# Deep cross network on one core: where the bias vectors are loaded and summed, and the first and third input transposes in column tiles

## The chip, the cores and the metric

One core of a Trainium2 chip runs the whole kernel. The metric is the device time of one execution in microseconds (us). The time given for a kernel is the median of its runs; the profile comes from one of those runs.

## The reference

```python
    B, F, D, L = 4096, 26, 16, 6
    Din = min(F * D, 1024)
...
        "x0": _w((lambda *s: _rng.normal(s) * 0.05)(B, Din)),
        "ws": _w((lambda *s: _rng.normal(s) * 0.05)(L, Din, Din)),
        "bs": _w((lambda *s: _rng.normal(s) * 0.05)(L, Din)),
...
def reference(x0, ws, bs):
    x = x0
    for l in range(ws.shape[0]):
        x = x0 * (x @ ws[l] + bs[l]) + x
    return x
```

So `x0` has 4096 rows of 416 features, and six layers each take a 416 x 416 product, add a bias, multiply by `x0` and add the layer's input. All tensors are bf16.

## The kernel before, in words

The 4096 rows are worked through in four stages of 1024 rows (`NS`), each in two halves of 512 (`H`), and for each stage in six layers (`L`). The work is kept transposed: features on partitions, rows along the free dimension. The 416 features are three full chunks of 128 (`NC`) and a tail of 32 (`DR`), whose rows lie four groups deep on the partitions. In PSUM the products of all layers so far add up, so a layer's result is `x0` times (the sum in the bank plus the sum of the biases up to that layer). These sums of the biases, for every layer at once, are what `cb_sb` holds.

Every engine has its own order of work, written out by hand, and the engines meet at semaphores. The order at the start of the program, around the change:

- TensorE runs 40 warm-up matmuls on a constant (L130), in groups of four 128x32 column tiles. Then `bias_sums` (L295 to L303) waits for the load of the biases and multiplies `bsa_sb` (a row of ones and six rows of biases) by the triangular `u_sb`: 16 small matmuls into bank 1. Then `fill(1)` adds four more warm-up matmuls. The loop at L308 transposes the first two pairs of 128-row blocks of x, three chunks each, in the order `IN_ORDER`: 12 full 128x128 transposes (L312) into bf16 views of PSUM banks (`psT`).
- In the first layer of the first stage (`n == 0`, L355 to L367) the matmuls run chunk by chunk, `k` outside and `m` inside. `before_a` waits until the transposed inputs have been copied to SBUF. At `k == 0, m == 1` TensorE waits until `cb_sb` has been copied out of bank 1. At `k == 2, m == 1` it transposes the tail features (`tail_inputs`) and the third pair of blocks (`third_input`), both as ordinary matmuls by the identity in column tiles, with float32 results. The matmuls at L265 are all those that go through the helper `tile_mm`.
- Then come the row matmuls of the tail (L393 and L409), for which TensorE waits on the copies of the third input (`s_inD`, `s_inA`), on the copied tail (`s_te`) and on the small weights `wt_sb` and `wc_sb`.
- VectorE first clears `wc_sb` and writes the ones of `bsa_sb` (L141, L142), then copies the bias sums to `cb_sb` (L506), the first inputs' chunks 0 and 2 (L512), and chunks 0 and 2 of the third input (L517).
- ScalarE (ACT) copies chunk 1 of each (L561, L578) and the tail inputs (L576).
- Loads: SP's queue issues the biases (L134), the first and the third pair of x blocks (L135, L136), later a DMA transpose of the fourth pair (L158) and the weights. ACT's queue issues the second pair of x blocks (L137), the first layer's weights (L138), the tail features of the fourth pair (L139) and two pieces of `wt_sb`. GpSimd's queue (POOL) builds the identity and `u_sb` (L211, L215) and then issues two pieces of `wt_sb` (L125) and four of `wc_sb` (L206).

Semaphores that the steps below name: `s_bs` (biases landed), `s_zero` (VectorE's memsets), `s_set` (identity and `u_sb`), `s_xin` (x blocks landed), `s_inT` (a chunk transposed), `s_inD` and `s_inA` (a chunk copied by VectorE or ACT), `s_cbp` and `s_cb` (bias sums made and copied).

Of the kernel before, what the change touches and what calls it, by code (L numbers as in the profile page):

```python
# [8 lines left out]
ACTF = mybir.ActivationFunctionType  # L9


def bass_standalone__dcn_v2_cross__recsys_kernel(
# [8 lines left out]
    NC = 3  # L21
# [11 lines left out]
    with ExitStack() as es:  # L33
# [20 lines left out]
        o_sb = sb("o_sb", [128, NJ, D])  # L54
        ident = sb("ident", [128, 128])
        ones_sb = sb("ones_sb", [128, 256])
        bsa_sb = sb("bsa_sb", [L + 1, D])
        u_sb = sb("u_sb", [L + 1, L])
        cb_sb = sb("cb_sb", [128, NC + 1, L], FP32)
        cq_sb = sb("cq_sb", [128, NC + 2], FP32)  # L60
        ps = es.enter_context(nc.psum_tensor("ps", [128, 8, 512], FP32))
# [34 lines left out]


        IN_BANKS = ((3, 4, 6), (0, 5, 7))
        IN_ORDER = ((1, 0), (1, 1), (1, 2), (0, 0), (0, 1), (0, 2))
        THIRD = (3, 6, 7)  # L100

        NAT_BANKS = (0, 1, 2, 6, 7, 4, 3, 5)
# [23 lines left out]
                wt_sb[lane(g), a:b, 0:n1 - n0], ws[a:b, DF:D, n0:n1].rearrange("l p n -> p l n")  # L126
            ).then_inc(done, 16)

        for q in range(4 * 10):
            nc.tensor.matmul(  # L130
                ps[lane(q % 4), 7, 0:256], lhsT=CONST[:, 0:32], rhs=CONST, start=True, stop=True,
                skip_group_check=True, tile_position=(0, 32 * (q % 4)),
            )
        nc.sync.dma_start(bsa_sb[1:L + 1, :], bs[:, :]).then_inc(s_bs, 16)  # L134
        nc.sync.dma_start(xin_sb[:, 0:2, :], x0_w[:, 0, :, :]).then_inc(s_xin[0], 16)  # L135
        nc.sync.dma_start(xin_sb[:, 4:6, :], x0_w[:, 2, :, :]).then_inc(s_xin[2], 16)  # L136
        nc.scalar.dma_start(xin_sb[:, 2:4, :], x0_w[:, 1, :, :]).then_inc(s_xin[1], 16)  # L137
        nc.scalar.dma_start(w_sb[:, 0, :, :], wmain(0)).then_inc(s_w[0], 16)  # L138
        nc.scalar.dma_start(xtl_sb[:, :, :], x0_v[:, 6:JS, DF:D]).then_inc(s_xtl0, 16)  # L139
        nc.gpsimd.memset(ones_sb[:, :], 1.0).then_inc(s_ones, 1)  # L140
        nc.vector.memset(wc_sb[:, :, :], 0.0).then_inc(s_zero, 1)  # L141
        nc.vector.memset(bsa_sb[0:1, :], 1.0).then_inc(s_zero, 1)  # L142

        es2 = ExitStack()
# [57 lines left out]
        @block.gpsimd  # L202
        def _(pool):
            def load_wc(i, g):
                a, b = ((0, 1), (1, L))[i]
                pool.dma_start(  # L206
                    wc_sb[lane(g), a:b, 32 * g:32 * g + 32], ws[a:b, DF:D, DF:D].rearrange("l p n -> p l n")
                ).then_inc(s_wc[i], 16)

            pool.wait_ge(s_ones, 1)  # L210
            pool.affine_select(  # L211
                out=ident[:, :], in_=ones_sb[:, 0:128], pattern=[[-1, 128]],
                compare_op=ALU.is_equal, fill=0.0, base=0, channel_multiplier=1,
            ).then_inc(s_set, 1)
            pool.affine_select(  # L215
                out=u_sb[:, :], in_=ones_sb[0:L + 1, 0:L], pattern=[[1, L]],
                compare_op=ALU.is_ge, fill=0.0, base=1, channel_multiplier=-1,
            ).then_inc(s_set, 1)
            for g in (0, 2):
                load_wt(pool, g, 0, 1, s_wtp)  # L220
            pool.wait_ge(s_zero, 1)
            for i in range(2):
                for g in (1, 3):
                    load_wc(i, g)

            for s in range(NS):
                pool.wait_ge(s_te, s + 1)
                for l in range(L):
                    n = s * L + l + 1
                    if n == NL:  # L230
                        break
                    if n == 1:
                        pool.tensor_scalar(
                            out=cq_sb[:, 0:NC + 1], in0=cb_sb[:, :, L - 1], scalar1=-1.0, scalar2=None, op0=ALU.add
                        ).then_inc(s_cq, 1)
                        pool.wait_ge(s_cq, 1)
                        pool.tensor_tensor(
                            out=cq_sb[:, NC + 1:NC + 2], in0=cq_sb[:, NC:NC + 1], in1=cb_sb[:, NC, L - 2:L - 1], op=ALU.subtract
                        ).then_inc(s_cq, 1)
                    pool.wait_ge(s_ta, n)  # L240
                    dst = xot_sb[:, s, :] if l == L - 1 else xt_sb[:, (l + 1) % 2, 0:G]
                    pool.tensor_tensor(  # L242
                        out=dst, in0=t32_sb[:, n % 2, :], in1=x0t_sb[:, s, 0:G], op=ALU.mult
                    ).then_inc(s_xt, 1)
                    if n == NL - 1:
                        pool.tensor_scalar(
                            out=xot_sb[:, s, :], in0=t32_sb[:, n % 2, :], scalar1=cq_sb[:, NC + 1:NC + 2], scalar2=None, op0=ALU.add
                        ).then_inc(s_qt, 1)
                    if l == 2 and s > 0:
                        pool.wait_ge(s_ot, 16 * s)  # L250
                        pool.tensor_copy(
                            out=o_sb[:, (s - 1) * JS:s * JS, DF:D].rearrange("p (g r) f -> p r g f", r=2),
                            in_=ot_sb[:, s - 1, :, :].rearrange("p r (g f) -> p r g f", f=DR),
                        ).then_inc(s_otc, 1)
            pool.wait_ge(s_x0n, 16)
            for i, t in enumerate(POOL_TILES):
                pool.wait_ge(s_oA, i + 1)
                pool.tensor_tensor(
                    out=o_sb[:, j0 + t, :], in0=a32_sb[:, i, :], in1=x0n_sb[:, t, :], op=ALU.mult
                ).then_inc(s_oP, 1)  # L260

        @block.tensor
        def _(pe):
# [3 lines left out]
                    skip_group_check=True, tile_position=(0, 32 * q),  # L267
                )

            def fill(n):  # L270
                for i in range(n):
                    for q in range(4):
                        tile_mm(ps[lane(q), 7, 0:256], CONST[:, 0:32], CONST, q, True)

            def tail_inputs():
                for r in range(2):
# [7 lines left out]
            def third_input():  # L284
                pe.wait_ge(s_inD, 4)
                for c in range(NC):
                    for j in range(2):
                        for q in range(4):
                            f0 = c * 128 + 32 * q
                            ins = tile_mm(  # L290
                                ps[lane(q), THIRD[c], j * 128:j * 128 + 128], xin_sb[:, 4 + j, f0:f0 + 32], ident[:, :], q, True
                            )
                    ins.then_inc(s_inT, 1)

            def bias_sums():  # L295
                pe.wait_ge(s_bs, 16)
                pe.wait_ge(s_zero, 2)
                pe.wait_ge(s_set, 2)
                for c in range(NC + 1):
                    for q in range(4):  # L300
                        f0 = c * 128 + 32 * q if c < NC else DF
                        ins = tile_mm(ps[lane(q), 1, c * 8:c * 8 + L], bsa_sb[:, f0:f0 + 32], u_sb[:, :], q, True)
                ins.then_inc(s_cbp, 1)  # L303

            bias_sums()
            fill(1)
            pe.wait_ge(s_set, 1)
            for i, (h, c) in enumerate(IN_ORDER):  # L308
                if c == 0:
                    pe.wait_ge(s_xin[h], 16)  # L310
                for j in range(2 * h, 2 * h + 2):
                    ins = pe.transpose(  # L312
                        out=psT[:, IN_BANKS[h][c], (j % 2) * 128:(j % 2 + 1) * 128],
                        in_=xin_sb[:, j, c * 128:(c + 1) * 128], identity=ident[:, :],
                    )
                ins.then_inc(s_inT, 1)

            for s in range(NS):
                for l in range(L):
# [26 lines left out]

                    def before_a(k):
                        if n == 0:
                            pe.wait_ge((s_inD, s_inA, s_inD)[k], (3, 2, 4)[k])
                        else:  # L350
                            pe.wait_ge(s_xa, NC * (n - 1) + k + 1)
                            if l == 0 and k == 0:
# [2 lines left out]
                    if n == 0:  # L355
                        pe.wait_ge(s_w[0], 16)
                        for k in range(NC):
                            before_a(k)
                            for m in range(NC):
                                if k == 0 and m == 1:  # L360
                                    pe.wait_ge(s_cb, 1)
                                if k == 2 and m == 1:
                                    pe.wait_ge(s_xin[2], 16)
                                    pe.wait_ge(s_xtl0, 16)
                                    tail_inputs()
# [136 lines left out]

        @block.vector
        def _(dve):
            dve.wait_ge(s_cbp, 1)
            dve.tensor_copy(  # L506
                out=cb_sb[:, :, :], in_=ps[:, 1, 0:8 * (NC + 1)].rearrange("p (c e) -> p c e", e=8)[:, :, 0:L],
            ).then_inc(s_cb, 1)
            for i, (h, c) in enumerate(IN_ORDER):
                if c != 1:  # L510
                    dve.wait_ge(s_inT, i + 1)
                    dve.tensor_copy(  # L512
                        out=x0T_sb[:, c, h * 256:(h + 1) * 256], in_=psT[:, IN_BANKS[h][c], 0:256]
                    ).then_inc(s_inD, 1)
            for c in (0, 2):
                dve.wait_ge(s_inT, 2 * NC + c + 1)
                dve.tensor_copy(out=x0T_sb[:, c, 512:768], in_=ps[:, THIRD[c], 0:G]).then_inc(s_inD, 1)  # L517
            dve.wait_ge(s_cb, 1)
            for s in range(NS):
                for l in range(L):  # L520
# [35 lines left out]
        def _(act):  # L556
# [18 lines left out]
            act.wait_ge(s_tp, 1)  # L575
            act.activation(out=x0t_sb[:, 0, :], in_=ps[:, 5, :], func=ACTF.Copy).then_inc(s_te, 1)  # L576
            act.wait_ge(s_inT, 2 * NC + 2)
            act.activation(out=x0T_sb[:, 1, 512:768], in_=ps[:, THIRD[1], 0:G], func=ACTF.Copy).then_inc(s_inA, 1)  # L578
            act.wait_ge(s_cb, 1)
            for s in range(NS):  # L580
                for l in range(L):
# [77 lines left out]
```

## Time and profile before

| What | Value |
|---|---|
| Median of 8 runs | 128.27 us (127.9 to 129.09) |
| The profiled execution's own time | 129.09 us |
| Its span, first to last instruction | 127.8 us |
| PE busy | 124.3 us (97%) |
| VectorE (DVE) busy | 99.9 us (78%) |
| ScalarE (ACT) busy | 67.6 us (53%) |
| GpSimd (POOL) busy | 24.1 us (19%) |
| Warm-up matmuls, L130, 40 of them | 0.83 to 3.16 us |
| First 12 transposes, L312 | start 3.63 us, 1.46 us long |
| First layer's first matmuls, L265 | start 5.13 us |
| First row matmul, L393 | start 8.81 us |

The span counts from the first to the last instruction of the execution; what is left to its own time lies around it. PE is TensorE's matmuls, PEld its weight loads, which overlap them; a matmul's duration includes its way through the array, so several lie on top of each other. A group's line gives the line of the kernel, the engine, the operation, output and inputs with shapes, how often, and the busy time; a square bracket gives the idle time of the engine ahead of it and what ended it. The shape 128*32 is a matmul on a column tile of 32 columns, and four such tiles run side by side.

### The profile page before, as it was taken

To read this page: it belongs to the slowest core of one execution; us is meant where nothing else is said; L and a number is where in the kernel's file an instruction comes from. 1 tells how busy PE (TensorE), PEld (TensorE's weight loads), DVE (VectorE), ACT (ScalarE), POOL (GpSimd) and SP (SyncE) were. 2 spreads that over 40 slices of the span, in tenths; PEclk is the share of its full clock that TensorE was granted. 3 is DMA by queue.
4 is the path that set the end of the run, shared out by engine and by line. 5 is a ranking of instruction groups with operands and counts; after the bars stand their busy time and mean duration, and the time that the engine had idled before them with its cause. 6 is when DMAs were issued, how large, how long until landed. Compare 5 with 4: busy or idle time off the path is not lost.

```text
span 127.8 us, 5323 instructions
## 1 busy us (share of the span) xinstructions
PE 124.3 (97%) x2410; PEld 62.8 (49%) x2410; DVE 99.9 (78%) x154; ACT 67.6 (53%) x146; POOL 24.1 (19%) x44
## 2 busy tenths in 40 slices
PE   7999999999999999999999999999999999999991
PEld 5655445445445445445445454444444454454660
DVE  2329779789788798797797797797797797797973
ACT  0625555575744564575753573575762564566830
POOL 7512012022022023022022022121020120220441
DMA  3950799900009969450005889960006910430006
GB/s 110 269 133 5 161 241 241 152 5 0 5 3 48 213 100 232 116 204 5 0 5 111 155 115 233 313 215 0 5 0 47 206 24 0 155 117 5 0 25 246
DMA packets 31889, 13.49 MB, mean 106 GB/s; under 512 B 24950, under 2 KB 31868, under 8 KB 31868
## 3 DMA queue, kind: packets, MB, share of 16 engines
q1 hardware_dynamic: 30476, 12.12, 44.8%
q10 hardware_dynamic: 1200, 0.99, 2.4%
q8 instruction: 19, 0.31, 1.0%
q0 software_dynamic: 192, 0.06, 0.3%
q14 instruction: 2, 0.02, 0.0%
HBM read 3.86 MB, written 3.41 MB: 57 GB/s over the span
## 4 chain that ended last, share of the span: by engine, by line
PE 97%; DVE 0%; issue 0%
PE ps L265 82%; PE ps L393 10%; PE ps L130 2%; PE ps L449 2%; PE ps L312 1%; PE ps L464 1%; DVE o_sb L550 0%; PE ps L488 0%; PE ps L409 0%; PE ps L494 0%
## 5 line engine op out<-in xcount | busy, mean ns | idle before, releaser
L537 DVE SCALAR_TENSOR_TENSOR xT_sb<-ps,cb_sb,x0T_sb 128x512 bf16<-128x512 f32 x120 | 81.0, 744 | 16.4 <-PE ps L393 16.3
L265 PE MATMUL ps<-xT_sb,w_sb 128*32 128x512 bf16 (+1 forms) x1596 | 84.2, 364 | 0.0
L265 PEld LDWEIGHTS ps<-xT_sb,w_sb 128*32 128x32 bf16 x1596 | 41.0, 97 | 37.1 <-issue 4.0
L566 ACT ACTIVATE xt_sb<-xt_sb 32x256 bf16<-32x256 bf16 x76 | 31.5, 414 | 15.7 <-POOL xt_sb L242 15.1
L595 ACT ACTIVATE t_sb<-ps,cb_sb 64x256 f32<-64x256 f32 x46 | 21.5, 468 | 31.2 <-PE ps L265 30.9
L242 POOL TENSOR_TENSOR xt_sb<-t_sb,x0t_sb 128x256 bf16<-128x256 f32 x20 | 13.4, 672 | 81.4 <-ACT t_sb L595 81.4
L265 PE MATMUL ps<-x0T_sb,w_sb 128*32 128x512 bf16 (+1 forms) x336 | 19.5, 378 | 0.0
L537 DVE SCALAR_TENSOR_TENSOR xo_sb<-ps,cb_sb,x0T_sb 128x512 bf16<-128x512 f32 x18 | 12.1, 744 | 2.5 <-PE ps L393 2.5
L265 PEld LDWEIGHTS ps<-x0T_sb,w_sb 128*32 128x32 bf16 x336 | 8.9, 100 | 8.3 <-issue 2.1
L393 PE MATMUL ps<-xt_sb,wt_sb 32*128 32x512 bf16 x76 | 11.5, 380 | 0.0
L614 ACT ACTIVATE x0t_sb<-x_sb 32x512 bf16<-32x512 bf16 x12 | 7.5, 626 | 0.3
L409 PE MATMUL ps<-xt_sb,wt_sb 32*128 32x512 bf16 x38 | 7.4, 386 | 0.0
L393 PE MATMUL ps<-xt_sb,wc_sb 32*128 32x256 bf16 x76 | 7.3, 268 | 0.0
L393 PEld LDWEIGHTS ps<-xt_sb,wt_sb 32*128 32x128 bf16 x76 | 2.2, 92 | 8.1 <-DVE xT_sb L537 8.1
L393 PEld LDWEIGHTS ps<-xt_sb,wc_sb 32*128 32x128 bf16 x76 | 3.8, 93 | 2.2
L242 POOL TENSOR_TENSOR xot_sb<-t_sb,x0t_sb 128x256 bf16<-128x256 f32 x3 | 2.0, 674 | 12.6 <-ACT t_sb L595 12.6
L550 DVE SCALAR_TENSOR_TENSOR o_sb<-ps,x0n_sb 128x416 bf16<-128x416 f32 x6 | 3.3, 585 | 1.0 <-PE ps L494 0.9
L570 ACT ACTIVATE xo_sb<-ps,cq_sb 128x512 bf16<-128x512 f32 x5 | 3.3, 686 | 1.1 <-PE ps L393 1.1
L130 PE MATMUL ps<-const-bfloat16-1.0 128*32 128x256 bf16 x40 | 2.3, 418 | 0.8 <-PEq L644 0.8
L561 ACT ACT_TABLE_LOAD x1 | 1.3, 1283 | 3.3 <-issue 3.3
L517 DVE CAST x0T_sb<-ps 128x256 bf16<-128x256 f32 x2 | 0.8, 419 | 2.8 <-PE ps L265 2.8
L449 PE MATMUL ps<-w_sb,xT_sb 128*128 128x416 bf16 x12 | 2.8, 340 | 0.0
(52 smaller groups left out, 41.8 us busy)
## 6 DMA issues: line engine op xcount, KB each, us to landing
out_dram<-o_sb SPq DMA_DIRECT2D x2, 832.0 KB, 5.0
w_sb<-in_ws_dram SPq DMA_DIRECT2D x5, 312.0 KB, 3.4
x0n_sb<-in_x_dram SPq DMA_DIRECT2D x1, 832.0 KB, 5.4
out_dram<-o_sb SPq DMA_DIRECT2D x1, 624.0 KB, 4.1
out_dram<-o_sb SPq DMA_DIRECT2D x3, 208.0 KB, 2.0
xin_sb<-in_x_dram SPq DMA_DIRECT2D x2, 208.0 KB, 3.2
out_dram<-o_sb ACTq DMA_DIRECT2D x2, 208.0 KB, 2.0
w_sb<-in_ws_dram ACTq DMA_DIRECT2D x1, 312.0 KB, 3.6
```

Source lines behind the costliest of these rows:

```text
L130: nc.tensor.matmul(ps[lane(q % 4), 7, 0:256], lhsT=CONST[:, 0:32], rhs=CONST, start=True, stop=True, skip_group_check=True, tile_position= ...
L242: pool.tensor_tensor(out=dst, in0=t32_sb[:, n % 2, :], in1=x0t_sb[:, s, 0:G], op=ALU.mult).then_inc(s_xt, 1)
L265: return pe.matmul(dst, lhsT=lhsT, rhs=rhs, start=start, stop=True, skip_group_check=True, tile_position=(0, 32 * q),)
L393: return pe.matmul(dst, lhsT=lhsT, rhs=srct[lane(g), cols], start=l == 0 and start, stop=True, skip_group_check=True, tile_position=(32 * ...
L409: pe.matmul(ps[:, NC * h + 2, :], lhsT=wt_sb[lane(g), l, 0:128], rhs=srct[lane(g), :].rearrange("p (b r) -> p b r", b=2)[:, ::-1, :], star ...
L449: pe.matmul(ps[:, NAT_BANKS[t], 0:D], lhsT=xT_sb[:, (L - 1) % 2, k, rows], rhs=w_sb[:, L - 1, k, :], start=False, stop=True, skip_group_ch ...
L537: dve.scalar_tensor_tensor(out=dst, in0=ps[:, NC * half + c, :], scalar=cb_sb[:, c, l:l + 1], in1=x0T_sb[:, c, o:o + H], op0=ALU.add, op1= ...
L550: dve.scalar_tensor_tensor(out=o_sb[:, j0 + t, :], in0=ps[:, NAT_BANKS[t], 0:D], scalar=1.0, in1=x0n_sb[:, t, :], op0=ALU.add, op1=ALU.mul ...
L566: ins = act.activation(out=buf[lane(g), G:2 * G], in_=buf[lane(g ^ 1), 0:G], func=ACTF.Copy)
L570: act.activation(out=xo_sb[:, NS - 1, c, half * H:(half + 1) * H], in_=ps[:, NC * half + c, :], func=ACTF.Identity, bias=cq_sb[:, c:c + 1] ...
L595: ins = act.activation(out=t32_sb[HALVES[h], n % 2, :], in_=tail(h), func=ACTF.Identity, bias=cb_sb[HALVES[h], NC, l:l + 1],)
L614: ins = act.activation(out=x0t_sb[lane(g), s + 1, :].rearrange("p (b n) -> p b n", b=2), in_=src[:, ::-1, :] if g % 2 else src, func=ACTF. ...
```

## The change

- The biases are loaded by GpSimd's queue, ahead of its other six loads, instead of by SP's queue, where the load was first. GpSimd waits for VectorE's first memset before it.
- `bsa_sb` and `u_sb` have 128 rows instead of 7. VectorE clears all of `bsa_sb` first; its row of ones follows the clearing of `wc_sb`. Rows 7 to 127 of `bsa_sb` stay zero.
- SP's queue waits for that first memset before it issues the loads of x.
- Warm-up: 52 matmuls instead of 40, and `fill(1)` is gone.
- `bias_sums` stands behind the first transposes instead of ahead of them, writes to bank 5 instead of bank 1, and waits for ACT's first copy out of bank 5 as well.
- The first and the third transposes are transposes in 128x32 column tiles (`tile_tp`): 48 and 24 instructions, with bf16 results. Before, the first were 12 full transposes, and the third 24 ordinary matmuls with float32 results.
- `IN_ORDER` takes chunk 0 of the first pair third instead of fourth; the first layer's first matmuls wait for two of VectorE's copies instead of three.
- `tail_inputs`, `third_input` and the wait for `cb_sb` stand at `k == 2, m == 0`, one step earlier than the tail inputs stood before. The wait for `cb_sb` was at `k == 0, m == 1`.
- VectorE copies the bias sums after the first inputs instead of before them.

```diff
-        IN_ORDER = ((1, 0), (1, 1), (1, 2), (0, 0), (0, 1), (0, 2))
+        IN_ORDER = ((1, 0), (1, 1), (0, 0), (1, 2), (0, 1), (0, 2))
...
-        for q in range(4 * 10):
+        for q in range(4 * 13):
...
-        nc.sync.dma_start(bsa_sb[1:L + 1, :], bs[:, :]).then_inc(s_bs, 16)
+        nc.sync.wait_ge(s_zero, 1)
...
+        nc.vector.memset(bsa_sb[:, :], 0.0).then_inc(s_zero, 1)
         nc.vector.memset(wc_sb[:, :, :], 0.0).then_inc(s_zero, 1)
+        nc.vector.wait_ge(s_zero, 1)
         nc.vector.memset(bsa_sb[0:1, :], 1.0).then_inc(s_zero, 1)
...
+            pool.wait_ge(s_zero, 1)
+            pool.dma_start(bsa_sb[1:L + 1, :], bs[:, :]).then_inc(s_bs, 16)
             for g in (0, 2):
                 load_wt(pool, g, 0, 1, s_wtp)
-            pool.wait_ge(s_zero, 1)
+            pool.wait_ge(s_zero, 2)
...
+            def tile_tp(dst, src, q):
+                return pe.transpose(out=dst, in_=src, identity=ident[:, :], tile_position=(0, 32 * q))
...
-                            ins = tile_mm(
-                                ps[lane(q), THIRD[c], j * 128:j * 128 + 128], xin_sb[:, 4 + j, f0:f0 + 32], ident[:, :], q, True
+                            ins = tile_tp(
+                                psT[lane(q), THIRD[c], j * 128:j * 128 + 128], xin_sb[:, 4 + j, f0:f0 + 32], q
                             )
...
             def bias_sums():
                 pe.wait_ge(s_bs, 16)
-                pe.wait_ge(s_zero, 2)
+                pe.wait_ge(s_zero, 3)
                 pe.wait_ge(s_set, 2)
+                pe.wait_ge(s_inA, 1)
...
-            bias_sums()
-            fill(1)
             pe.wait_ge(s_set, 1)
             for i, (h, c) in enumerate(IN_ORDER):
                 if c == 0:
                     pe.wait_ge(s_xin[h], 16)
-                for j in range(2 * h, 2 * h + 2):
-                    ins = pe.transpose(
-                        out=psT[:, IN_BANKS[h][c], (j % 2) * 128:(j % 2 + 1) * 128],
-                        in_=xin_sb[:, j, c * 128:(c + 1) * 128], identity=ident[:, :],
-                    )
+                for j in range(2):
+                    for q in range(4):
+                        f0 = c * 128 + 32 * q
+                        ins = tile_tp(
+                            psT[lane(q), IN_BANKS[h][c], j * 128:j * 128 + 128], xin_sb[:, 2 * h + j, f0:f0 + 32], q
+                        )
                 ins.then_inc(s_inT, 1)
+            bias_sums()
...
-                            pe.wait_ge((s_inD, s_inA, s_inD)[k], (3, 2, 4)[k])
+                            pe.wait_ge((s_inD, s_inA, s_inD)[k], (2, 2, 4)[k])
...
-                                if k == 0 and m == 1:
+                                if k == 2 and m == 0:
                                     pe.wait_ge(s_cb, 1)
-                                if k == 2 and m == 1:
                                     pe.wait_ge(s_xin[2], 16)
```

VectorE's copy of the bias sums moves behind its loop over `IN_ORDER`, unchanged but for the bank, and the copies of the third input read `psT` instead of `ps`.

More of the change, by code (lines that the diff above doesn't have):

```diff
@@ L56, in bass_standalone__dcn_v2_cross__recsys_kernel @@
         ones_sb = sb("ones_sb", [128, 256])
-        bsa_sb = sb("bsa_sb", [L + 1, D])
-        u_sb = sb("u_sb", [L + 1, L])
+        bsa_sb = sb("bsa_sb", [128, D])
+        u_sb = sb("u_sb", [128, L])
         cb_sb = sb("cb_sb", [128, NC + 1, L], FP32)
@@ L215, in _ @@
             pool.affine_select(
-                out=u_sb[:, :], in_=ones_sb[0:L + 1, 0:L], pattern=[[1, L]],
+                out=u_sb[:, :], in_=ones_sb[:, 0:L], pattern=[[1, L]],
                 compare_op=ALU.is_ge, fill=0.0, base=1, channel_multiplier=-1,
             ).then_inc(s_set, 1)
+            pool.wait_ge(s_zero, 1)
+            pool.dma_start(bsa_sb[1:L + 1, :], bs[:, :]).then_inc(s_bs, 16)
             for g in (0, 2):
                 load_wt(pool, g, 0, 1, s_wtp)
-            pool.wait_ge(s_zero, 1)
+            pool.wait_ge(s_zero, 2)
             for i in range(2):
@@ L268, in tile_mm @@
                 )
[L270 to L273, printed above, removed]
+            def tile_tp(dst, src, q):
+                return pe.transpose(out=dst, in_=src, identity=ident[:, :], tile_position=(0, 32 * q))
             def tail_inputs():
@@ L301, in bias_sums @@
                         f0 = c * 128 + 32 * q if c < NC else DF
-                        ins = tile_mm(ps[lane(q), 1, c * 8:c * 8 + L], bsa_sb[:, f0:f0 + 32], u_sb[:, :], q, True)
+                        ins = tile_mm(ps[lane(q), 5, c * 8:c * 8 + L], bsa_sb[:, f0:f0 + 32], u_sb[:, :], q, True)
                 ins.then_inc(s_cbp, 1)
-            bias_sums()
-            fill(1)
             pe.wait_ge(s_set, 1)
@@ L504, in _ @@
         def _(dve):
[L505 to L508, printed above, removed]
             for i, (h, c) in enumerate(IN_ORDER):
@@ L514, in _ @@
                     ).then_inc(s_inD, 1)
+            dve.wait_ge(s_cbp, 1)
+            dve.tensor_copy(
+                out=cb_sb[:, :, :], in_=ps[:, 5, 0:8 * (NC + 1)].rearrange("p (c e) -> p c e", e=8)[:, :, 0:L],
+            ).then_inc(s_cb, 1)
             for c in (0, 2):
                 dve.wait_ge(s_inT, 2 * NC + c + 1)
-                dve.tensor_copy(out=x0T_sb[:, c, 512:768], in_=ps[:, THIRD[c], 0:G]).then_inc(s_inD, 1)
+                dve.tensor_copy(out=x0T_sb[:, c, 512:768], in_=psT[:, THIRD[c], 0:G]).then_inc(s_inD, 1)
             dve.wait_ge(s_cb, 1)
@@ L577, in _ @@
             act.wait_ge(s_inT, 2 * NC + 2)
-            act.activation(out=x0T_sb[:, 1, 512:768], in_=ps[:, THIRD[1], 0:G], func=ACTF.Copy).then_inc(s_inA, 1)
+            act.activation(out=x0T_sb[:, 1, 512:768], in_=psT[:, THIRD[1], 0:G], func=ACTF.Copy).then_inc(s_inA, 1)
             act.wait_ge(s_cb, 1)
```

## The prediction

> **What bounds the kernel now.** I read the page first: busy time by engine, then the chain that ended last.
>
> ```profile
> PE 124.3 (97%) x2410; PEld 62.8 (49%) x2410; DVE 99.9 (78%) x154; ACT 67.6 (53%) x146; POOL 24.1 (19%) x44
> ...
> PE 97%; DVE 0%; issue 0%
> ```
>
> TensorE carries the whole chain. From about 9.4 us on nothing that the diff touches runs (each of the 23 layers in the chain takes 4.87 us, and their code is the same), so the change is worth what it moves the moment at which TensorE gets through the first layer's row matmuls. Next the chain in order of time, for the start alone (start, duration, what):
>
> ```profile
> 0.83 2.33 PE ps L130 x31
> 3.16 0.53 PE ps L265 x14
> 3.69 1.39 PE ps L312 x12
> 5.09 0.05 issue
> 5.13 3.68 PE ps L265 x75
> 8.81 0.37 PE ps L393
> ```
>
> The warm-up matmuls end at 3.16, the bias sums and one more warm-up group fill the time to 3.62, twelve transposes run to 5.09, and the first layer's matmuls start at 5.13. The first x rows (issued by ACT at 0.80, landed 2.6 us later, about 3.4) are there by then: TensorE never waits for long. Third, the weight loads in order of time, which show TensorE's pace (four loads are one group of four column tiles, streaming 512 columns side by side):
>
> ```profile
> 5.10 0.17 PEld L265 LDWEIGHTS ps<-x0T_sb,w_sb 128*32 128x32 bf16 x8 [0.28 <-DMA w_sb<-in_ws_dram]
> 5.52 0.18 PEld L265 LDWEIGHTS ps<-x0T_sb,w_sb 128*32 128x32 bf16 x4 [0.25 <-issue]
> 5.95 0.18 PEld L265 LDWEIGHTS ps<-x0T_sb,w_sb 128*32 128x32 bf16 x4 [0.25 <-issue]
> 6.37 0.18 PEld L265 LDWEIGHTS ps<-x0T_sb,w_sb 128*32 128x32 bf16 x4 [0.25 <-issue]
> 6.80 0.18 PEld L265 LDWEIGHTS ps<-x0T_sb,w_sb 128*32 128x32 bf16 x4 [0.25 <-issue]
> 7.21 0.11 PEld L265 LDWEIGHTS ps<-x0T_sb,w_sb 128*32 128x32 bf16 x4 [0.23 <-issue]
> 7.43 0.11 PEld L265 LDWEIGHTS ps<-ident,xin_sb 128*32 128x32 bf16 x3
> ...
> 8.78 0.09 PEld L393 LDWEIGHTS ps<-x0t_sb,wt_sb 32*128 32x128 bf16 x1 [0.47 <-DVE x0T_sb L517]
> ```
>
> The pitch is 0.427 us until 6.80 and 0.21 after 7.21: TensorE doubles its pace at about 7.2. The last line is a true stall: the eight matmuls before it start at 8.20 and stream for 2 x 0.21, so the array is empty from 8.63 to 8.81, waiting for VectorE's float32 cast of the third input.
>
> Last, the busy time in two stretches (stretch, length, PE busy), and the DMA issues of the start (KB each, us from issue to landing):
>
> ```profile
> 0.37:3.78 3.41, 2.95 (x62) 2.09 (x63) 1.04 (x3) 0.51 (x1) 3.04 (x11) 1.00 0.55 167
> 3.78:7.20 3.42, 3.37 (x32) 1.93 (x34) 1.09 (x4) 1.50 (x3) 1.24 (x3) 1.00 0.94 227
> ```
>
> ```profile
> wt_sb<-in_ws_dram POOLq DMA_DIRECT2D x2, 16.0 KB, 4.3
> wt_sb<-in_ws_dram ACTq DMA_DIRECT2D x2, 8.0 KB, 4.1
> wc_sb<-in_ws_dram POOLq DMA_DIRECT2D x2, 2.0 KB, 4.0
> wc_sb<-in_ws_dram POOLq DMA_DIRECT2D x2, 10.0 KB, 3.4
> ```
>
> Small loads from GpSimd's queue land 3.4 to 4.3 us after issue. The bias on SP's queue was issued at 0.80, first of all, and the bias matmuls ran at 3.09, right behind the warm-up: it cost no wait.
>
> [...]
>
> **Part by part.**
> *Warm-up and transposes.* Before, 40 matmuls, the bias sums and 4 more reach 3.63. After, 52 in 13 groups: three groups more than 40, 3 x 0.21 = 0.64 behind 2.95 (where the 40 stop streaming), so 3.6.[...] The 48 tile transposes are 12 groups of four; the nearest row, the 40 tile matmuls on the same operands from 7.64 to 8.20, gives 0.056 a group at full clock and so 0.107 at half, what a full transpose costs now (1.39 for 12, tail included). So they stop streaming at 4.87. Bound from above: tiles in transpose mode run one after another, (48 - 12) x 0.107 = 3.9 us more; from below nothing.
> *SP's queue.* The wait on VectorE's first memset (start 0.97, 208 words at the 0.46 per 480 of the wc memset: done at 1.17) stands where the bias issue stood (0.39 long); the x issues go out at about 1.2 as before (1.25). Cost 0, within 0.05.
> *GpSimd's queue.* The bias load goes out first, at 1.6, and takes 0.5 to 0.76 us; all six later loads move back by as much. wt then lands near 2.9 + 4.3 = 7.2 and the first wc near 3.9 + 4.0 = 7.9. They are needed at about 8.6 and 9: hidden. If TensorE came 0.9 us sooner they would bind.
> *The bias.* It now lands at 1.6 plus 3.3 to 4.4 (the shortest and longest from this queue): 4.9 to 6.0. I take 5.5: smaller than wt, but behind the same full engines. TensorE comes to the wait at 4.87, and ACT's copy of the bank, also waited for, ends at 4.95. Queued behind it in TensorE's order is everything: the first layer's matmuls. They wait 0.6, then wake-up 0.1 and the bias sums 0.2 (3.09 to 3.29): start at 5.8 instead of 5.13, 0.67 late. Ends: 0.1 late (landed at 4.9) and 1.2 late (6.0).
> *The third input.* bf16 tiles make VectorE's casts 0.29 instead of 0.42, and 12 matmuls (0.64) instead of 8 stand between the tiles and the rows. The 0.18 stall goes; the next in line is ACT's pair of copies (0.60 + 0.38), which leaves 0.12 to 0.18 of gain.
> *Sum.* In the profiled execution (129.09, span 127.8, so 1.3 around it; the slowest of the eight shown, 0.8 over the median) the first 1.4 us of the late stream run at half clock, so half of the 0.67 comes back when the clock rises at 7.2: +0.33 - 0.15 = +0.2. If the clock is up by 5.1 (which I infer for a run of 127.9, as nothing else here differs by 1.2 us), none comes back: +0.67 - 0.15 = +0.5. Over the runs +0.4, so 128.27 + 0.4 = 128.7.
>
> **The rivals.**
> A, the forecast: TensorE waits for the bias, 128.4 to 129.2, chance 0.40. Half a per cent, 0.64 us, is about what a measurement can tell from no change; A lies on both sides of it (0.22 within, 0.18 slower).
> B: the wait also delays the clock.[...] Where most runs fall so, the median is about 130.1.[...] 0.27.
> C, not slower: the bias lands by 4.95. Then the sums cost 0.2 and the third input gives 0.15 to 0.2 back[...]: 128.2. It decides wholly at 4.95. For it: six rows in all, first in its queue; against: no GpSimd load landed within 3.3 us. 0.17 (0.13 within, 0.04 faster).
> D, faster: [...]the clock up by 3.8 in nearly every run: all become like the fastest, 127.9, less the stall of 0.18 and a cast's 0.13: 127.6. It decides only if the bias too is there by 4.95. 0.12.
> E: tile transposes don't run side by side: 128.3 + 3.9, about 132. 0.04.
>
> **Numbers.** Slower 0.18 + 0.27 + 0.04 = 0.49; within 0.22 + 0.13 = 0.35; faster 0.04 + 0.12 = 0.16. The range leaves out D and E and reaches over C and B: 127.9 to 130.2.
>
> **What would show it.** After the transposes an idle stretch of TensorE that ends with the bias load, bias matmuls at 5.5 to 5.7, the first layer's from 5.8; no idle ahead of the row matmuls; the pace doubling at 7.2 or earlier (A) or past 8.5 (B). I am wrong if the bias matmuls start before 5.1 (C, D), if the transposes take longer than 1.4 us (E), or if GpSimd's later loads end the wait of the row matmuls.

## The result, and the profile after

| | before | changed |
|---|---|---|
| Median | 128.29 us (32 runs, 127.9 to 131.07) | 130.96 us (11 runs, 129.11 to 133.13) |
| Ratio | | 1.0123, interval 1.0086 to 1.016 |
| Span, median | 127.1 us (47 runs of a later series) | 129.75 us (12 runs, the profiled one among them; 127.5 to 131.5) |
| Time around the span, median | 1.24 us (the same 47) | 1.56 us (the same 12) |
| The profiled execution | 129.09, span 127.8 | 131.88, span 130.3 |

The change makes the kernel slower by 1.2%: 0.0123 x 128.29 = 1.6 us, between 1.1 and 2.05 us. The comparison leaves out executions more than 1.5% above a kernel's fastest, five of the eleven here and the profiled one with them, so the ratio is smaller than that of the medians (130.96 - 128.29 = 2.7 us), and for what it rests on I read a second profile of the same kernel (131.86 us median in that second series), an execution with a span of 127.7 us.

First the changed kernel's page: busy time by engine, and the chain that ended last.

```profile
PE 124.6 (96%) x2454; PEld 63.6 (49%) x2454; DVE 99.9 (77%) x155; ACT 67.6 (52%) x146; POOL 24.6 (19%) x45
...
PE 92%; DMA 4%; POOL 1%; DVE 0%; issue 0%; POOLq 0%
```

TensorE is still the engine with the work (0.3 us more of it), but it no longer carries the whole chain: 4% is a transfer. The chain in order of time names it (start, duration, what):

```profile
0.79 0.32 POOL ones_sb L140
1.57 5.67 DMA bsa_sb<-in_bs_dram
7.29 3.13 PE ps L269 x55
10.41 0.34 PE ps L275 x23
10.75 0.65 PE ps L269 x12
11.39 0.32 PE ps L395
11.94 4.33 PE ps L269 x84
```

The chain starts on GpSimd, goes through the bias load, and reaches TensorE only at 7.29. The row matmuls stand at 11.39 where they stood at 8.81 (their first record is at 11.33); from there on every layer takes what it took. TensorE's own records show the wait in the brackets (start, duration, then idle time and what ended it), and the weight loads show the pace:

```profile
3.56 1.52 PE L275 MATMUL ps<-ident,xin_sb 128*32 128x128 bf16 x48
7.29 0.28 PE L269 MATMUL ps<-u_sb,bsa_sb 128*32 128x6 bf16 x16 [2.21 <-DMA bsa_sb<-in_bs_dram]
7.47 2.72 PE L269 MATMUL ps<-x0T_sb,w_sb 128*32 128x512 bf16 x24
```

```profile
9.13 0.18 PEld L269 LDWEIGHTS ps<-x0T_sb,w_sb 128*32 128x32 bf16 x4 [0.25 <-issue]
9.56 0.17 PEld L269 LDWEIGHTS ps<-ident,xin_sb 128*32 128x32 bf16 x3 [0.25 <-issue]
...
10.18 0.39 PEld L275 LDWEIGHTS ps<-ident,xin_sb 128*32 128x32 bf16 x24
```

The pitch of a group is 0.43 us until 9.98 and half of that afterwards. So in this execution two things are late: the first layer's start, by 2.3 us (7.47 against 5.13), and the doubling of the pace, which came at 7.2 before.

Now the second profile, the shorter execution, in order of time:

```profile
1.57 4.11 DMA bsa_sb<-in_bs_dram
5.68 0.04 issue
5.72 1.65 PE ps L269 x40
7.37 0.02 issue
7.40 0.42 PE ps L269 x16
7.81 0.34 PE ps L275 x24
8.15 0.65 PE ps L269 x12
8.79 0.32 PE ps L395
```

and TensorE's records of the same:

```profile
3.56 1.00 PE L275 MATMUL ps<-ident,xin_sb 128*32 128x128 bf16 x48
5.72 0.26 PE L269 MATMUL ps<-u_sb,bsa_sb 128*32 128x6 bf16 x16 [1.16 <-DMA bsa_sb<-in_bs_dram]
5.89 1.48 PE L269 MATMUL ps<-x0T_sb,w_sb 128*32 128x512 bf16 x24
7.40 0.24 PE L269 MATMUL ps<-ident,xin_sb 128*32 128x128 bf16 x3
```

Here TensorE is at the doubled pace, which I call full clock, already in the transposes (1.00 us instead of 1.52), the bias lands at 5.68, and TensorE waits 1.16 us for it. The row matmuls start at 8.73 (their first record; the chain has 8.79). A second gap follows: 24 matmuls are six groups of 0.213, done at 5.89 + 1.28 = 7.17, and the next start at 7.40. No releaser is named, but the loads' times tell it (KB, us from issue to landing):

```profile
bsa_sb<-in_bs_dram POOLq DMA_DIRECT2D x1, 4.9 KB, 4.1
xtl_sb<-in_x_dram ACTq DMA_DIRECT2D x1, 16.0 KB, 5.6
x0T_sb<-in_x_dram SPq DMA_TRANSPOSE x1, 5.1
```

The tail features `xtl_sb`, which TensorE needs next, took 5.6 us instead of 4.0 before: issued at 1.70, they landed at 7.25, and TensorE goes on at 7.40. The third x blocks, also waited for there, had landed at 5.34.

### The profile page after: what moved, and what is told of

Same layout as the page of the kernel before. It is cut to its first block, busy times and chain, and to the rows that moved or that the text cites. A ratio compares the mean times of both kernels' runs of the same rounds, so it can differ in the third digit from the quotient of the medians.

```text
span 130.3 us, 5414 instructions
## 1 busy us (share of the span) xinstructions
PE 124.6 (96%) x2454; PEld 63.6 (49%) x2454; DVE 99.9 (77%) x155; ACT 67.6 (52%) x146; POOL 24.6 (19%) x45
## 4 chain that ended last, share of the span: by engine, by line
PE 92%; DMA 4%; POOL 1%; DVE 0%; issue 0%; POOLq 0%
PE ps L269 80%; PE ps L395 10%; DMA bsa_sb<-in_bs_dram 4%; PE ps L451 2%; PE ps L466 1%; DVE o_sb L552 0%; PE ps L490 0%; PE ps L275 0%; POOL ones_sb L140 0%; POOL ident L213 0%; PE ps L411 0%; POOL u_sb L217 0%; PE ps L496 0%; POOLq L646 0%
## 5 line engine op out<-in xcount | busy, mean ns | idle before, releaser
L130 PE MATMUL ps<-const-bfloat16-1.0 128*32 128x256 bf16 x52 | 3.0, 419 | 0.8 <-PEq L646 0.8
L578 ACT ACTIVATE x0t_sb<-ps 128x512 bf16<-128x512 f32 x1 | 0.6, 597 | 5.2 <-PE ps L269 5.2
L510 DVE COPY x0T_sb<-ps 128x256 bf16<-128x256 bf16 x4 | 1.1, 292 | 2.3 <-PE ps L275 2.0
```

Source lines behind the costliest of these rows:

```text
L130: nc.tensor.matmul(ps[lane(q % 4), 7, 0:256], lhsT=CONST[:, 0:32], rhs=CONST, start=True, stop=True, skip_group_check=True, tile_position= ...
```

## The experiments

My theory after the result: the bias load on GpSimd's queue is the whole loss, through its late landing. The rivals: the tile transposes cost it; the order (bias sums and third input moved) costs it; the late clock is the larger part; something outside the span costs it. Below, "changed" is the changed kernel and "before" the one before; each diff is against the kernel named.

### The load put back

Changed, with everything of the bias load as before: first on SP's queue, seven rows, nothing cleared, no wait of SP's queue (in part).

```diff
-        nc.sync.wait_ge(s_zero, 1)
+        nc.sync.dma_start(bsa_sb[1:L + 1, :], bs[:, :]).then_inc(s_bs, 16)
...
-            pool.wait_ge(s_zero, 1)
-            pool.dma_start(bsa_sb[1:L + 1, :], bs[:, :]).then_inc(s_bs, 16)
```

> The changed kernel with the bias load as it was before: first on SP's queue, seven rows, no clearing of 128 rows, GpSimd's queue one load shorter; sums behind the transposes, tiles, warm-up and orders as changed. Late load: no wait for the bias; what is left is the tiles' and the order's cost, ratio 0.999 to 1.004; the time around the span falls back from 1.5 to 1.7 us to 1.2 to 1.3. Rival 'order' (sums behind the transposes): 1.006 or more.

Measured: 128.72 us, ratio 1.0006 (0.9987 to 1.0024); time around the span 1.31. TensorE at the bias matmuls and at the rows:

```profile
5.09 0.26 PE L265 MATMUL ps<-u_sb,bsa_sb 7*32 7x6 bf16 x16 [0.54 <-ACT x0T_sb L559]
5.28 1.48 PE L265 MATMUL ps<-x0T_sb,w_sb 128*32 128x512 bf16 x24
...
7.90 0.39 PE L391 MATMUL ps<-x0t_sb,wt_sb 32*128 32x512 bf16 x1
```

The whole loss is gone, with tiles, warm-up and order as changed. It also times the delay at the start: against the shorter execution above, at the same full clock, the first layer is 0.61 earlier (5.28 against 5.89) and the rows 0.83 (7.90 against 8.73), which is 0.61 plus the gap of 0.23. But that lead doesn't reach the end: twice later in this execution the 84 matmuls of a layer, which take 4.33 us elsewhere, take 4.71 and 4.58, with no releaser named, and the two spans, 127.5 and 127.7, differ by 0.2. So the 0.83 is what the first layer lost, not what the execution lost. The landing itself differs more: on SP's queue, issued at 0.80, the last step of `s_bs` came at 2.54 (2.19 in the kernel before). What stays is a wait for ACT's first copy, which the bracket names.

### Without tiles

Changed, with full-width first transposes and the third input as ordinary matmuls again (in part; the copies follow).

```diff
-                            ins = tile_tp(
-                                psT[lane(q), THIRD[c], j * 128:j * 128 + 128], xin_sb[:, 4 + j, f0:f0 + 32], q
+                            ins = tile_mm(
+                                ps[lane(q), THIRD[c], j * 128:j * 128 + 128], xin_sb[:, 4 + j, f0:f0 + 32], ident[:, :], q, True
...
-                for j in range(2):
-                    for q in range(4):
...
+                for j in range(2 * h, 2 * h + 2):
+                    ins = pe.transpose(
```

> The changed kernel with the tile transposes undone: the first 12 are full-width transposes again and the third input goes through ordinary matmuls with float32 results; the bias stays on GpSimd's queue and its sums behind the transposes. Late load: as slow as the changed kernel, ratio 1.008 to 1.018, with a wait of TensorE for the bias of 0.6 us or more. Tiles: back to the kernel before, ratio 0.998 to 1.003.

Measured: 129.46 us, ratio 1.0074 (1.005 to 1.0098); time around the span 1.50.

```profile
6.13 0.26 PE L269 MATMUL ps<-u_sb,bsa_sb 128*32 128x6 bf16 x16 [1.37 <-DMA bsa_sb<-in_bs_dram]
```

The wait and most of the loss stay without a single tile transpose, so the tiles aren't needed for it. The loss is a little smaller than the changed kernel's, and than the 1.008 expected; the intervals of the two ratios overlap.

### The bias sums moved behind the wait

Changed, with the bias sums behind the tail inputs, in bank 4; the load itself, the cleared 128 rows and the wait of SP's queue stay (in part; the waits on `cb_sb` move with it).

```diff
-            bias_sums()
...
                                     tail_inputs()
+                                    bias_sums()
                                     third_input()
```

> The changed kernel with the bias sums one stretch later: not behind the first transposes but in the first layer, behind the tail inputs (some 2 to 3 us later), into bank 4; the bias stays on GpSimd's queue. Late load: the first layer's matmuls start at about 5.1, the wait for the bias is gone or under 0.3 us, time 127.9 to 128.4, ratio 0.996 to 1.001. If the load lands past 7 in many runs, some of it remains, up to 1.005. Rival 'queue' (GpSimd's six later loads, moved back, bind instead): the wait moves to the row matmuls, ratio 1.005 or more.

Measured: 129.1 us, ratio 1.0063 (1.0037 to 1.0089); spans 127.2 to 128.5, median 127.4; around the span 1.70. The first layer starts at 5.16, and the wait is elsewhere. The chain, then TensorE at the rows:

```profile
2.31 0.56 POOL wt_sb L125
2.88 5.16 DMA wt_sb<-in_ws_dram
8.18 0.37 PE ps L395
```

```profile
8.18 0.37 PE L395 MATMUL ps<-x0t_sb,wt_sb 32*128 32x512 bf16 x1 [0.16 <-DMA wt_sb<-in_ws_dram]
```

The ratio is over the expected 0.996 to 1.001, but the span comes back to within 0.3 us of before's 127.1, so the wait for the bias was nearly all that the change cost inside the span, and clearing the 128 rows costs no more than these 0.3 us there. What remains, 0.46 of the 0.8 us that the ratio stands for, lies around the span. And once TensorE isn't held up, GpSimd's later load `wt_sb` binds, as the rival 'queue' had it, but by 0.16 us only.

### A spare load on GpSimd's queue

Before, with a second load of the same biases at the head of GpSimd's queue, into a buffer that no computation reads; GpSimd waits for it late in the program.

```diff
+            pool.dma_start(spare_sb[1:L + 1, :], bs[:, :]).then_inc(s_spare, 16)
             for g in (0, 2):
```

> The kernel before with one load more: GpSimd's queue first brings the biases to a spare tile that nothing reads (its landing is waited for on GpSimd near the end). It measures what a load at the head of GpSimd's queue costs with nobody waiting for it: the time around the span should grow from 1.25 to about 1.5 us if that load makes it, and the six later loads should land some 0.5 us later without binding. Ratio 1.000 (nothing outside the span) to 1.003 (0.3 us around the span). If GpSimd's later loads bind, over 1.004.

Measured: 128.68 us, ratio 1.0021 (1.0001 to 1.0041); span median 127.15, time around the span 1.50 (1.45 to 1.54) against 1.24 (1.19 to 1.34). The span doesn't move, the time outside it grows by 0.26 us: that part of the loss needs no wait at all. Why a load of GpSimd costs there, no trace shows, since it lies outside what the profiler records.

### The load on SP's queue, between the x blocks

Changed, with the load issued by SP behind the first x blocks instead of by GpSimd.

```diff
         nc.sync.dma_start(xin_sb[:, 0:2, :], x0_w[:, 0, :, :]).then_inc(s_xin[0], 16)
+        nc.sync.dma_start(bsa_sb[1:L + 1, :], bs[:, :]).then_inc(s_bs, 16)
...
-            pool.wait_ge(s_zero, 1)
-            pool.dma_start(bsa_sb[1:L + 1, :], bs[:, :]).then_inc(s_bs, 16)
```

> The changed kernel, but the bias load goes out on SP's queue, between the first and the third x blocks (about 1.6 us), instead of on GpSimd's. Theory 'late load' (TensorE waits for the bias that GpSimd's queue brings too late, and the rest of the change costs nothing): the load lands by about 3.5 to 4.5, TensorE has no wait of over 0.2 us behind the transposes, time 128.0 to 128.4, ratio to the kernel before 0.997 to 1.002. Rival 'order' (sums behind the transposes cost by themselves): 128.8 or more. Rival 'tiles' (tile transposes cost): 128.8 or more, with transposes longer than 1.4 us.

Measured: 129.33 us, ratio 1.0056 (1.003 to 1.0081), around the span 1.30. The wait for the bias is gone (first layer at 5.24), but the third x blocks went out behind it, at 2.04, and took 6.23 us:

```profile
8.51 0.24 PE L268 MATMUL ps<-ident,xin_sb 128*32 128x128 bf16 x3 [1.80 <-DMA xin_sb<-in_x_dram]
```

My edit made a new wait, so the ratio says nothing of the old one; the load put back at the head of the queue settled that. But its landing compares the queues more nearly: issued at 1.62, about when GpSimd issued it, the load landed at 4.87, after 3.25 us, where GpSimd's took 4.1 and 5.7, and the same load at the head of SP's queue 1.4 to 1.7. So in these single executions part of the late landing goes with being behind the x loads, on SP's queue too, and part with GpSimd's queue. The run does confirm, without GpSimd's seventh load, that the time around the span falls back to 1.30.

### The load as GpSimd's first instruction

Changed, seven rows, no clearing, no wait ahead of the load (in part).

```diff
+        nc.gpsimd.dma_start(bsa_sb[1:L + 1, :], bs[:, :]).then_inc(s_bs, 16)
         nc.gpsimd.memset(ones_sb[:, :], 1.0).then_inc(s_ones, 1)
...
-            pool.dma_start(bsa_sb[1:L + 1, :], bs[:, :]).then_inc(s_bs, 16)
```

> The changed kernel with the bias load as GpSimd's very first instruction (seven rows, so that nothing has to be cleared first), at about 0.8 us instead of 1.57; the x loads of SP still wait for VectorE's first memset. If the landing is a fixed time after the issue (4.1 us in the second look at the changed kernel), the bias lands at about 4.9, the wait is gone, and the ratio falls to 1.002 to 1.004 (the time around the span stays 0.3 us longer). If the engines' other loads set it (the bias's data move at 4.85 to 4.92 in the changed kernel's trace, when the x and weight loads are through), it still lands at 5.6 or later and the ratio stays over 1.008.

Measured: 129.98 us, ratio 1.0131 (1.008 to 1.0182). It doesn't answer the question. GpSimd begins the load at 1.34, only 0.23 us before the 1.57 of the changed kernel, and it lands 4.5 us later, at 5.86. But VectorE's first memset now takes 0.42 us, so SP's x loads start at 1.37 instead of 1.17, and the first x blocks land at 5.40 instead of about 3.9 (GpSimd's other loads moved too, so that the 0.2 us alone did it isn't shown):

```profile
5.45 0.63 PE L272 MATMUL ps<-ident,xin_sb 128*32 128x128 bf16 x32 [1.21 <-DMA xin_sb<-in_x_dram]
```

### The tiles and the third input alone

Three kernels from before: both tile transposes; the third in tiles only; that one with tail and third input a step earlier (`m == 0`). In part:

```diff
-                            ins = tile_mm(
+                            ins = tile_tp(
...
-                                if k == 2 and m == 1:
+                                if k == 2 and m == 0:
```

> The kernel before with the tile transposes alone (first and third input); bias load, sums, warm-up, orders and waits as before. Late load: 0.05 to 0.2 us faster than before, from the shorter casts of the third input, ratio 0.998 to 1.001. Tiles: ratio 1.005 or more.

> The kernel before with the third input alone in tile transposes with bf16 results (24 instructions for 24). The prediction's step: shorter casts, 0.29 instead of 0.42 us, so the row matmuls wait less: 0.05 to 0.13 us faster, ratio 0.999. If the 0.3 us of the kernel with both tile transposes came from the third input: ratio 1.002 or more.

> As the kernel with the third tile transposes alone, and the tail and third inputs one step earlier, as in the changed kernel (12 matmuls instead of 8 ahead of the row matmuls). The prediction's step: the stall of 0.18 us ahead of the first row matmul goes, 0.12 to 0.18 us faster than the kernel before, ratio 0.9985 to 0.999; this would be the fastest of all here. If the loads bind instead, 1.000.

Measured: both 128.69 us, 1.0025 (1.0009 to 1.0041); the third alone 128.24 us, 0.9993 (0.9976 to 1.001); a step earlier 128.72 us, 1.0015 (0.9989 to 1.0041). So the third in tiles can't be told from no change, and both together cost some 0.3 us, which I didn't expect and don't explain: in that profile the first 48 tiles take 1.48 us from 3.49, as priced. That the first tiles make it isn't shown: the intervals of the two ratios just meet, and the load put back, with both tile transposes, stands at 1.0006. In the kernel a step earlier the next limit shows in the bracket, the DMA transpose of the fourth blocks:

```profile
8.92 0.73 PE L265 MATMUL ps<-x0T_sb,w_sb 128*32 128x256 bf16 x16 [0.32 <-DMA x0T_sb<-in_x_dram]
```

None of them beats the kernel before.

### The clock: filling the wait, a shorter warm-up, and the kernel again

Changed with 32 more warm-up matmuls (bank 1) ahead of `bias_sums`; changed with 44 warm-ups instead of 52; and the changed kernel unedited.

```diff
+            for i in range(4 * 8):
+                tile_mm(ps[lane(i % 4), 1, 0:256], CONST[:, 0:32], CONST, i % 4, True)
             bias_sums()
```

```diff
-        for q in range(4 * 13):
+        for q in range(4 * 11):
```

> The changed kernel with 32 more warm-up matmuls (into bank 1) between the first transposes and the bias sums, so that TensorE is kept busy for 0.9 us (full clock) to 1.7 us (half clock) of its wait. Theory 'late load' alone: they fill idle time and change nothing, ratio 1.008 to 1.016. Theory 'clock'[...]: the runs with the latest ends go, ratio 1.004 to 1.008, with the pace doubled before the first layer's matmuls.

> The changed kernel with 44 warm-up matmuls instead of 52. Late load with a held-up tail: in the changed kernel's traces the 16 kB instruction fetch starts at 5.2 us and the completions of all loads stop from about 5.8 to 7.2.[...] the bias then lands by about 6 in nearly every run and the longest runs go: median 129.2 to 129.8, ratio 1.006 to 1.010. If the fetch stays at 5.2, the spread stays: median 130.5 or more.

> The changed kernel as it is, for a second look at its spread. Late load: TensorE waits for the bias until about 5.7 to 6.1 in the shorter runs, and until about 7.2 in the longer ones[...]. Ratio near 1.012; spans from 127.5 up.

Measured, six runs each: filled 130.52 us, 1.0124 (1.0071 to 1.0177), spans 127.6 to 129.8; 44 warm-ups 131.2 us, 1.0121 (1.0048 to 1.0194), 127.5 to 130.0; again 131.86 us, 1.0236 (1.0179 to 1.0292), 127.7 to 131.6. Neither edit lowers the ratio below the first comparison's 1.0123, though the 44 warm-ups were expected to reach 1.006 to 1.010. The kernel again lies above the filled one in the same series, but four of its six runs are of 131.8 to 133.1 us, and the shortest of the two are alike (129.28 and 129.12); with six runs each, whether filling the wait helps isn't settled.

The profiles part the two delays. Filled: bias late at 7.21, full clock behind it (24 matmuls are six groups of 0.213 and the way through the array). 44 warm-ups: bias earlier at 6.02, but half pace to the third input. The lines, one fence for each:

```profile
7.26 0.26 PE L269 MATMUL ps<-u_sb,bsa_sb 128*32 128x6 bf16 x16 [0.95 <-DMA bsa_sb<-in_bs_dram]
7.47 1.48 PE L269 MATMUL ps<-x0T_sb,w_sb 128*32 128x512 bf16 x24
```

```profile
6.07 0.28 PE L269 MATMUL ps<-u_sb,bsa_sb 128*32 128x6 bf16 x16 [1.16 <-DMA bsa_sb<-in_bs_dram]
6.25 2.75 PE L269 MATMUL ps<-x0T_sb,w_sb 128*32 128x512 bf16 x24
```

The rows start at 10.09 filled and at 10.86 with 44 warm-ups, against 8.73 in the shorter execution of the changed kernel: 1.4 us late by the landing alone, 2.1 by the half pace and a landing 0.34 later. Both executions have spans of 129.8 us; the filled one loses another 0.8 in one layer near 89 us, with no releaser named. With both delays the first profile's rows start at 11.33. These are single executions at the long end of their kernels: they show that each delay occurs, not what it cost the runs that the ratio compares. No profile was had of an execution of the changed kernel between 127.7 and 130.3.

## Why the prediction was right, and where it was too small

It said slower, by a wait for the bias load, and that holds: putting the load back removes the whole loss. The size was 0.4 us against a measured 1.6 (1.1 to 2.05); 128.29 + 1.6 = 129.9 is inside the range but 1.2 us over the forecast, and the plain median of the changed kernel, 130.96, is above the range's end of 130.2. That 129.9 is inside is in part luck: the range reached so far up for rival B's late clock, which isn't shown to make the loss of the compared runs. By its own steps:

*Warm-up and transposes.* Held, and with it the tiles run side by side: 48 in 1.52 us at half pace. That is over the 1.4 us named as a sign of E, but it includes the way through the array, as the 1.46 us of the twelve transposes before did; one after another would have been 3.9 us more. Rival E is refuted.

*SP's queue.* Held: the x loads are issued at 1.17. But "within 0.05" may have been the condition of it: in the kernel with the load first the x loads went out 0.2 us later and the first blocks landed 1.5 us later.

*The bias.* The term of the sum that was mis-sized. The prediction took a landing at 5.5, and 6.0 as the late end; measured were 5.68 and 7.24 in the changed kernel's two profiles, and 6.02, 6.09 and 7.21 with 44 warm-ups, without tiles and with the wait filled. The wait was 1.16 us in the shorter execution, not 0.6, partly because TensorE, already at full clock, arrived sooner (its transposes end at 4.56, not 5.08). The bias matmuls began 0.04 us after the landing (5.68 to 5.72); the wake-up of 0.1 in the prediction was an estimate. The first layer started at 5.89 (predicted 5.8), or at 7.47. The mistake behind the late end was to take the landings of GpSimd's other loads before (3.4 to 4.4 us) as bounds for this one. The trace of the first profile shows where the time went: TensorE waits until `s_bs` stands at sixteen; thirteen of the sixteen steps had come by 5.70, and the last three came at 7.22 to 7.24, 1.5 us later. What held those three back the trace doesn't show.

*GpSimd's later loads.* "Hidden", unless TensorE came sooner: it comes sooner in the kernel with later bias sums, and there `wt_sb` binds by 0.16 us, landing at 8.04 and not 7.2.

*The third input.* Predicted to gain 0.12 to 0.18; the tiles alone can't be told from nothing (0.9993), nor with the step earlier (1.0015). In the changed kernel's shorter execution the array still stands empty between the last of three groups begun at 7.95 (7.95 + 0.64 = 8.59) and the rows at 8.73: 0.14 instead of 0.18.

*What the sum lacked.* The time around the span (from 1.24 to 1.56; the spare load alone adds 0.26 of these 0.32), and the held-up tail features (0.23). For an execution of the shorter kind the terms add up: spans of 127.5 to 127.7 against 127.1, and 0.32 around, give 0.7 to 0.9. The rest of the 1.6 comes from the executions between, with spans of 128.7 to 129.5 us; what these wait for was not seen.

*Rival B.* Seen, in part: half pace to 9.98 in the first profile and to the third input with 44 warm-ups. What raises the pace no run here shows, and that rival's 130.1 was an estimate of mine. In the first profile TensorE stood empty for 2.21 us, and the pace doubled 2.69 us after work began again (7.29 to 9.98). In the kernel before TensorE was busy for 6.32 of the 6.37 us from 0.83 on, and the pace doubled only at 7.2. In the shorter execution, of the same kernel as the first profile, it had doubled by the end of the transposes at 4.56. Nor is it shown that the clock makes the loss of the compared runs. C falls with the wait, D came true for the clock in the shorter execution and lost it again to the wait.

## What to carry to other kernels

A tiny load that TensorE needs at the start goes out first, ahead of the large ones: here its six rows landed 1.4 to 1.7 us after issue at the head of SP's queue, where they cost nothing that could be measured (1.0006), 3.25 us behind the first x blocks on the same queue, and 4.1 and 5.7 us on GpSimd's. Don't bound a landing by other loads of the same queue (GpSimd's took 3.3 to 4.4 us before), and ask what each later load does when something ahead of it goes out a few tenths later: 0.4 us more at the issue of the third x blocks went with 2.9 us more at their landing. Compare the time around the span as well as the span, for an edit can cost there (0.26 us with the spare load) without a trace of it in the profile.

## What the hardware showed that I had not expected

In five profiles (the changed kernel twice, later sums, filled wait, load between the x blocks) the loads move only 7 to 42 GB/s from 6.4 to 6.8 us. Stretch, length, busy times, granted clock, share of DMA busy and GB/s; first the shorter execution of the changed kernel:

```profile
5.60:6.00 0.40, 0.28 (x20) 0.28 (x24) 0.00 (x0) 0.00 (x0) 0.00 (x0) 1.00 1.15 150
6.00:6.40 0.40, 0.40 (x12) 0.20 (x11) 0.18 (x1) 0.00 (x0) 0.00 (x0) 1.00 3.81 136
6.40:6.80 0.40, 0.40 (x16) 0.21 (x12) 0.00 (x0) 0.00 (x0) 0.00 (x0) 1.00 0.08 7
6.80:7.20 0.40, 0.40 (x12) 0.08 (x4) 0.00 (x0) 0.00 (x0) 0.00 (x0) 1.00 0.08 10
7.20:7.60 0.40, 0.38 (x20) 0.23 (x20) 0.00 (x0) 0.00 (x0) 0.00 (x0) 1.00 1.10 224
```

then the kernel with the load put back:

```profile
6.40:6.80 0.40, 0.40 (x24) 0.29 (x20) 0.00 (x0) 0.00 (x0) 0.00 (x0) 1.00 1.07 212
6.80:7.20 0.40, 0.40 (x44) 0.40 (x35) 0.05 (x1) 0.14 (x1) 0.00 (x0) 1.00 0.70 160
```

Read the last column: 7 and 10 GB/s against 212 and 160. The late completions of the bias and of the tail features, 7.2 to 7.3, fall at the end of that hole. With 44 warm-ups there was no such hole (113 and 101 GB/s).

One thing that stands near the hole in the first profile is a packet of 16 KB on the queue that the profile calls "instruction", from 5.25 to 6.44; in the kernel before, with 174 and 160 GB/s in the same two stretches, that packet starts at 8.11. That it makes the hole isn't shown: the two only stand side by side. In the kernel with the spare load the loads also move only 41 GB/s from 6.4 to 6.8, and with the load as GpSimd's first instruction 11 to 25 GB/s from 5.6 to 6.8. What makes the hole stays open, as do the 0.3 us of the two tile transposes.

The column of the granted clock reads 1.00 in all these stretches, and also from 6.50 to 9.90 in the first profile, where the pace was half: the half pace at the start is seen only in the pitch of the weight loads and of the matmuls.
